# Chunked attention and a squared-ReLU feed-forward on one core: another order of the transfers in the SP queue, and of the attention steps between matmuls

## The chip, the core and the metric

The kernel runs on one core of a Trainium2 chip. The metric is the time of one execution on the device, in microseconds (us); the runs of the kernel before are 8, with a median of 291.59 us (286.88 to 293.01).

## The reference, cut to what matters

Attention is computed in chunks of 64 positions, each chunk for itself; its output, read as 4608 tokens of 512 values, goes through a feed-forward layer with a squared ReLU.

```python
# q, k, v: (8, 8, 576, 64) = batch, heads, positions, head_dim; chunk = 64
scores = matmul(q_c, k_c.T) / 8
attn = exp(scores - max(scores)); attn = attn / (sum(attn) + 1e-9)
x = matmul(attn, v_c)            # per chunk; then as (B*S, H*D) = (4608, 512)
h = maximum(x @ w_in, 0.0)       # w_in: (512, 2048)
out = (h * h) @ w_out            # w_out: (2048, 512)
```

## The kernel before

**Groups and blocks.** A group is four chunks (256 tokens), a block two groups (512 tokens): 18 groups, 9 blocks; block j holds groups 2j and 2j+1. Sixteen groups are "whole": their four chunks come from one batch row. Each batch row has nine chunks, so the ninth ones are left over, and they make groups 14 and 15 (block 7, the "rests").

**Loads** (`pieces`, L522, with `qk_pieces`, L99, and `v_pieces`, L139). A whole group's q and k come in four pieces of 256 KB (q and k of each half); a rest group's in eight of 128 KB. Its V comes as even heads (`ve_sb`) and odd heads (`vo_sb`): for a pair of whole groups 9 pieces of 64 or 128 KB, for the pair of rests 16 of 64 KB. `pieces(far)` hands out first all q and k of both groups, then all V: 17 pieces for a whole pair, 32 for the rests. All these loads are issued by SP, one after the other, and SP also issues the two kinds of DMA transposes; it goes through its queue in order, and an instruction that waits for a semaphore holds those behind it. The stores of the output are issued by POOL (L440).

**Attention of a group**, as steps that the plan places:
- C (`cast_qk`, L232): q and k cast to bf16, for these groups on ACT (L237), when their load has landed.
- TD (`transpose_qk_dma`, L239): a DMA transpose on SP, `qkT<-qkb`, 512 KB; it waits for C.
- SC (`scores`, L247): 32 small matmuls (L257) from qkT into a PSUM tile `ps_att` (two buffers), then the exponential on ACT (L264).
- AV (`values`, L267): per half of the group 16 small matmuls with V (L281) into a `ps_att` tile, then on DVE a reciprocal (L288) and a product (L289) that makes `x`.
- XT (`transpose_x`, L295): from group 6 on a DMA transpose on SP, `xT<-x`, 256 KB (L302); it waits for `x`.

**The feed-forward of a block.** `ffn_in` (L337) makes 16 tiles of `gT`, each from four matmuls 128x512 (L344) with `xT` of the block; ACT takes the ReLU (L355), DVE the square (L359), three of the 16 squares are on ACT (L357). `ffn_out` (L377) computes the second product by seven half-sized products instead of eight, in 14 halves (L412), with differences and sums on DVE (L372) and a few copies on ACT (L456, L465, L492).

**The order.** It is written out by hand, by slots. A slot is one turn of a generator: 0 to 15 the tiles of `ffn_in`, 16 to 29 the halves of `ffn_out`. While block j is multiplied, the attention of block j+1 (`nxt`) is done from SC on, and for block j+2 (`far`) the loads, C and TD. After a slot's matmuls are issued, first one more piece is loaded if the slot is in `go_slots`, then come the steps that the plan has there (`slots`); pieces that are left over are loaded at the block's end. Slots give the order in each engine's queue, not times: SP runs as far ahead as its waits allow.

Blocks 0 and 1 have plans of their own (L572 to L594). For j from 2 on (L595 to L610): one piece after each slot from 0 on; SC of both groups after slot 5, AV after 8 and 11, XT after 11 and 14, C after 18 and 22, TD after 20 and 24. Block 3 has SC after 6, AV after 9 and 12, XT after 12 and 15. Block 2 also loads the V of block 3 first (26 pieces in all), and has SC after 8 and 10, AV after 12 and 15, XT after 15 and 18, C after 20 and 23, TD after 22 and 25.

Of the kernel before, what the change touches and what calls it, by code (L numbers as in the profile page):

```python
# [17 lines left out]
def kernel(  # L18
# [80 lines left out]
    def qk_pieces(g):  # L99
        q_sb = in_pool.tile([128, 2, H, D], FP32, name="q_sb")  # L100
        k_sb = in_pool.tile([128, 2, H, D], FP32, name="k_sb")
        qk[g] = (q_sb, k_sb)
        if g < FIRST_DMA_T:
            b, s = chunks[g][0]
            for dst, src in ((q_sb, q), (k_sb, k)):
                yield lambda dst=dst, src=src, b=b, s=s: nc.sync.dma_start(
                    out=dst.rearrange("p t h d -> p (t h d)").rearrange(
                        "p (h e) -> p h e", h=H),
                    in_=src[b, :, s:s + GT, :].rearrange("h (s i) d -> s h (i d)", i=2))
            return  # L110
        for t, p, m, b, s in runs(g):
            for dst, src in ((q_sb, q), (k_sb, k)):
                yield lambda dst=dst, src=src, b=b, s=s, t=t, p=p, m=m: nc.sync.dma_start(
                    out=dst[p:p + m, t, :, :],
                    in_=src[b, :, s:s + m, :].rearrange("h s d -> s h d"))
# [23 lines left out]
    def v_pieces(g):  # L139
        for t, p, m, b, s in runs(g):  # L140
            yield lambda t=t, p=p, m=m, b=b, s=s: nc.sync.dma_start(
                out=v_even[g % NV][p:p + m, t, :, 0:D],
                in_=v[b, 0::2, s:s + m, :].rearrange("h s d -> s h d"))
        for n, p, m, b, s in odd_loads[g]:
            yield lambda n=n, p=p, m=m, b=b, s=s: nc.sync.dma_start(
                out=v_odd[n % NO][p:p + m, :, 0:D],
                in_=v[b, 1::2, s:s + m, :].rearrange("h s d -> s h d"))

    def go(pieces):
        for f in pieces:  # L150
            f()
# [163 lines left out]
    C, TD = cast_qk, transpose_qk_dma  # L315
    SC, AV, XT = scores, values, transpose_x
# [20 lines left out]
    def ffn_in(j, parts):  # L337
        if j not in gTs:
            gTs[j] = ffn_pool.tile([128, n_ft, BT], BF16, name="gT")
        gT, xT = gTs[j], xTs[j]  # L340
        for u, (c, n, ft) in enumerate((c, n, ft) for c, n, fts in parts for ft in fts):
            h = ps_ffn.tile([128, 512], FP32, name="ps_ffn")
            for dt in range(n_dt):
                nc.tensor.matmul(  # L344
                    out=h[:, 0:n],
                    lhsT=w_in_bf[:, dt, ft * 128:(ft + 1) * 128],
                    rhs=xT[:, c // 128:(c + n) // 128, dt, :],
                    start=(dt == 0), stop=(dt == n_dt - 1))
            if j < 3:
                if n == 512 or u % 2 == 0:  # L350
                    rl_tile = ffn_pool.tile([128, 512], FP32, name="rl", bufs=3).bitcast(BF16)
                rl = rl_tile[:, u % 2 * 512:] if n < 512 else rl_tile
            else:
                rl = ffn_pool.tile([128, 512], FP32, name="rl", bufs=3)
            nc.scalar.activation(out=rl[:, 0:n], in_=h[:, 0:n], func=AF.Relu)  # L355
            if (n == 512 and ft in SQUARES_ON_ACT) or (n < 512 and ft in (12, 3)):
                nc.scalar.activation(out=gT[:, ft, c:c + n], in_=rl[:, 0:n], func=AF.Square)  # L357
            else:
                nc.vector.tensor_tensor(  # L359
                    out=gT[:, ft, c:c + n], in0=rl[:, 0:n], in1=rl[:, 0:n], op=ALU.mult)  # L360
            yield
# [12 lines left out]
    def sum_quarters(out, in0, in1, op=ALU.add, half=slice(None)):  # L374
        return lambda _: add(nc.vector, out[:, half], in0[:, half], in1[:, half], op)
# [119 lines left out]
    def ffn_out_by_ft(j):  # L495

        gT = gTs.pop(j)
        n_tt = len(blocks[j]) * GT // 128
        o_ps = [ps_ffn.tile([128, d_model], FP32, name="ps_ffn") for _ in range(n_tt)]

        def mm(tt, ft):
            nc.tensor.matmul(  # L502
                out=o_ps[tt],
                lhsT=gT[:, ft, tt * 128:(tt + 1) * 128],
                rhs=w_out_bf[:, ft, :],
                start=(ft == 0), stop=(ft == n_ft - 1))

        for ft in range(n_ft - 4):
            for tt in range(n_tt):
                mm(tt, ft)  # L510
            yield
        for tt in range(n_tt):
            for ft in range(n_ft - 4, n_ft):
                mm(tt, ft)
            o_sb = ffn_pool.tile([128, d_model], FP32, name="o_sb", bufs=4)
            nc.scalar.copy(out=o_sb, in_=o_ps[tt])
            b, s0 = chunks[blocks[j][tt // 2]][0]
            t0 = b * S + s0 + tt % 2 * 128
            nc.gpsimd.dma_start(out=out[t0:t0 + 128, :], in_=o_sb)
            yield  # L520

    def pieces(grps):  # L522
        for g in grps:
            yield from qk_pieces(g)
        for g in grps:
            yield from v_pieces(g)
# [37 lines left out]
    for j, grps in enumerate(blocks):  # L564
        nxt = blocks[j + 1] if j + 1 < len(blocks) else []
        far = blocks[j + 2] if j + 2 < len(blocks) else []
        plan = {}

        def at(slot, f, g):
            plan.setdefault(slot, []).append((f, g))  # L570

        if j == 0:  # L572
            loads, go_slots = pieces(far), range(17)
            at(28, sum_quarters(b11_p_b21, b11, b21), None)
            for slot, f in ((24, TA), (27, SC), (29, AV), (31, XT)):
                at(slot, f, nxt[0])
            at(31, TQ, nxt[1])
            at(31, sum_quarters(b11_m_b22, b11, b22, ALU.subtract), None)
            phases = [ffn_in(0, [(0, 512, range(n_ft))]), ffn_out_by_ft(0)]
        elif j == 1:  # L580
            loads, go_slots = itertools.chain(*map(qk_pieces, far)), range(26, 48)
            for slot, f in ((1, TK), (4, SC), (7, AV), (12, XT)):
                at(slot, f, grps[1])
            for i, g in enumerate(nxt):
                for slot, f in ((16 + 4 * i, C), (21 + 4 * i, TD), (36 + i, SC), (38 + 2 * i, AV),
                                (41 + 2 * i, XT)):
                    at(slot, f, g)
            for i, g in enumerate(far):
                at(36 + 4 * i, C, g)
                at(42 + 3 * i, TD, g)  # L590
            at(2, sum_quarters(b11_p_b12, b11, b12), None)
            at(12, sum_quarters(b12_p_b22, b12, b22), None)
            at(20, sum_quarters(b21_p_b22, b21, b22), None)
            phases = [ffn_in(1, [(0, 256, FT_ORDER), (256, 256, FT_ORDER)]), ffn_out(1)]  # L594
        else:  # L595
            loads, go_slots = pieces(far), range(32)
            slots = {SC: (5, 5), AV: (8, 11), XT: (11, 14), C: (18, 22), TD: (20, 24)}
            if j == 3:
                slots.update({SC: (6, 6), AV: (9, 12), XT: (12, 15)})
            if j == 2:  # L600
                loads = itertools.chain(*map(v_pieces, nxt), loads)
                slots = {SC: (8, 10), AV: (12, 15), XT: (15, 18), C: (20, 23), TD: (22, 25)}
                go_slots = [*range(18), *range(26, 32)]
            for f in (SC, AV, XT):
                for i, g in enumerate(nxt):
                    at(slots[f][i], f, g)
            for f in (C, TD):
                for i, g in enumerate(far):
                    at(slots[f][i], f, g)
            phases = [ffn_in(j, [(0, BT, FT_ORDER)]), ffn_out(j)]  # L610
        slot = 0
        for phase in phases:
            for _ in phase:
                if slot in go_slots:
                    for f in loads:
                        f()
                        break
                for f, g in plan.get(slot, []):
                    f(g)
                slot += 1  # L620
        assert all(x < slot for x in plan), (j, slot, sorted(plan))
        go(loads)
# [30 lines left out]
```

## Time and profile before

| | |
|---|---|
| median of 8 runs | 291.59 us (286.88 to 293.01) |
| the profiled execution | 291.19 us, its span 289.4 us |
| PE, DVE, ACT busy in the span | 94%, 65%, 56% |
| granted TensorE clock, mean | 0.997 |
| packets on the hardware queue of SP | 47.33 MB, 76.9% of 16 engines' span |
| packets on POOL's queue (stores) | 9.18 MB, 9.7% |
| qkT by DMA: issue on SP, least / median / most | 1.4 / 2.9 / 4.4 us |
| qkT by DMA: from issue to landing | 3.9 / 5.9 / 8.7 us |
| xT by DMA: issue on SP | 1.2 / 1.3 / 3.5 us |
| xT by DMA: from issue to landing | 3.0 / 3.3 / 6.0 us |

How to read the lines of the profile. In a list of waits a line gives who waited, `<-`, for what, then the total in us, the number of times and the longest. In order of time, a line gives the start from the span's beginning, the time, the engine (SPq and ACTq are an engine's queue), the line of the kernel, the operation, output `<-` inputs, how many were merged, and in brackets the idle time before it and what ended that. A DMA's time there is that of its issue; the landing is asked for separately. The row of digits beside DMA cuts the span into 40 slices of 7.2 us, 9 being 90% busy or more.

### The profile page before, as it was taken

How to read it: one execution, taken by the hardware profiler on the slowest of the kernel's cores; microseconds unless marked ns; L12 is line 12 of the kernel's file. 1: busy time of each engine (PE TensorE's matmuls, PEld its weight loads, DVE VectorE, ACT ScalarE, POOL GpSimd, SP SyncE). 2: the span in 40 equal slices, each digit the busy share in tenths (PEclk: the TensorE clock that was granted, in tenths of full speed). 3: DMA queues.
4: the chain of work that ended last, by engine and by line, in shares of the span. 5: the costliest groups of instructions: out<-in, count | busy, mean ns of one | idle time of the engine just before them, and what ended most of it. 6: DMA issues, size and time to landing. Idle time of an engine off the chain costs nothing.

```text
span 289.4 us, 7298 instructions
## 1 busy us (share of the span) xinstructions
PE 271.0 (94%) x3011; PEld 179.8 (62%) x3014; DVE 187.8 (65%) x305; ACT 161.7 (56%) x270; POOL 54.4 (19%) x89
## 2 busy tenths in 40 slices
PE   2999999999999999799699999999999999999994
PEld 1774444788774586348544784478448844884583
DVE  1157505898943694289546974697479647965792
ACT  1527705794358654866167637763876387308710
POOL 2037733150161002000300021002000200051012
PEclk9999999999999999999999999999999999999998
DMA  7999999999999999999999999588899951132003
GB/s 204 235 332 358 321 333 251 299 217 204 215 208 268 198 191 254 194 196 206 224 247 211 200 219 269 99 154 205 235 229 192 192 164 39 39 71 75 2 18 128
DMA packets 156369, 57.10 MB, mean 197 GB/s; under 512 B 139504, under 2 KB 152048, under 8 KB 156336
## 3 DMA queue, kind: packets, MB, share of 16 engines
q1 hardware_dynamic: 153296, 47.33, 76.9%
q0 software_dynamic: 2896, 9.18, 9.7%
q8 instruction: 23, 0.38, 0.6%
q10 hardware_dynamic: 144, 0.13, 0.1%
q14 instruction: 10, 0.08, 0.1%
HBM read 36.70 MB, written 9.44 MB: 159 GB/s over the span
## 4 chain that ended last, share of the span: by engine, by line
PE 38%; DVE 5%; ACT 4%; DMA 2%; issue 2%; ACTq 0%
PE ps_ffn L412 21%; PE ps_ffn L344 16%; ACT rl L355 3%; DVE gT L359 2%; DMA xT<-x 2%; DVE x L289 2%; ACT e L264 2%; PE ps_att L281 0%; DVE rec L288 0%; DVE o_sb L492 0%; ACTq L355 0%; ACT gT L357 0%
## 5 line engine op out<-in xcount | busy, mean ns | idle before, releaser
L344 PE MATMUL ps_ffn<-xT,w_in_bf 128*128 128x512 bf16 (+1 forms) x640 | 129.8, 358 | 3.4 <-DMA xT<-x 3.2
L359 DVE TENSOR_TENSOR gT<-rl 128x512 bf16<-128x512 f32 (+2 forms) x132 | 74.4, 594 | 66.3 <-ACT rl L355 65.1
L355 ACT ACTIVATE rl<-ps_ffn 128x512 f32<-128x512 f32 (+2 forms) x160 | 85.9, 553 | 34.1 <-PE ps_ffn L344 31.2
L344 PEld LDWEIGHTS <-w_in_bf 128*128 128x128 bf16 x640 | 60.6, 98 | 60.9 <-DMA xT<-x 2.9
L412 PEld LDWEIGHTS <-w_st 128*128 128x128 bf16 x640 | 62.0, 98 | 7.6 <-DVE w_st L372 0.2
L372 DVE TENSOR_TENSOR w_st<-gT 128x2048 bf16<-128x2048 bf16 x40 | 47.3, 1218 | 0.2
L412 PE MATMUL ps_ffn<-w_out_bf,w_st 128*128 128x256 bf16 x384 | 45.1, 273 | 0.0
L440 POOL DMA_DIRECT2D out_dram<-o_sb x25 | 17.8, 714 | 132.3 <-DVE o_sb L372 127.7
L412 PE MATMUL ps_ffn<-w_sum,w_st 128*128 128x256 bf16 x256 | 29.6, 273 | 0.0
L412 PEld LDWEIGHTS <-gT 128*128 128x128 bf16 x256 | 25.0, 98 | 4.3
L289 DVE TENSOR_TENSOR x<-ps_att,rec 128x512 bf16<-128x512 f32 x36 | 24.9, 691 | 1.2
L492 ACT COPY o_sb<-ps_ffn 128x512 f32<-128x512 f32 (+1 forms) x8 | 4.5, 558 | 32.4 <-PE ps_ffn L412 32.4
L264 ACT ACTIVATE e<-ps_att 128x1024 bf16<-128x1024 f32 x18 | 17.9, 1021 | 6.6 <-PE ps_att L257 6.6
L357 ACT ACTIVATE gT<-rl 128x512 bf16<-128x512 f32 (+2 forms) x28 | 16.8, 599 | 0.9
L412 PE MATMUL ps_ffn<-w_sum,gT 128*128 128x256 bf16 x128 | 15.3, 273 | 0.0
L412 PE MATMUL ps_ffn<-w_out_bf,gT 128*128 128x256 bf16 x128 | 15.3, 273 | 0.0
L502 PE MATMUL ps_ffn<-w_out_bf,gT 128*128 128x512 bf16 x61 | 14.3, 379 | 0.6 <-ACT rl L355 0.3
L281 PEld LDWEIGHTS <-e 64*64 64x64 bf16 x576 | 6.9, 107 | 9.0 <-DVE x L289 3.5
L159 POOL CAST w_in_bf<-w_st 128x1024 bf16<-128x1024 f32 (+1 forms) x9 | 8.6, 967 | 19.6 <-DMA w_st<-in_moe_w_in_dram 19.6
L237 ACT CAST qkb<-k_sb 128x1024 bf16<-128x1024 f32 x10 | 10.5, 1046 | 1.5 <-DMA k_sb<-in_k_dram 1.5
L237 ACT CAST qkb<-q_sb 128x1024 bf16<-128x1024 f32 x10 | 10.5, 1049 | 1.4 <-DMA q_sb<-in_q_dram 1.4
L281 PE MATMUL ps_att<-ve_sb,e 64*64 64x65 bf16 x288 | 9.5, 197 | 1.9 <-DVE x L289 1.7
(52 smaller groups left out, 160.4 us busy)
## 6 DMA issues: line engine op xcount, KB each, us to landing
out_dram<-o_sb POOLq DMA_DIRECT2D x29, 256.0 KB, 4.6
q_sb<-in_q_dram SPq DMA_DIRECT2D x24, 256.0 KB, 5.1
k_sb<-in_k_dram SPq DMA_DIRECT2D x24, 256.0 KB, 4.9
ve_sb<-in_v_dram SPq DMA_DIRECT2D x32, 128.0 KB, 3.8
w_st<-in_moe_w_in_dram SPq DMA_DIRECT2D x8, 512.0 KB, 7.3
w_st<-in_moe_w_out_dram SPq DMA_DIRECT2D x8, 512.0 KB, 6.1
vo_sb<-in_v_dram SPq DMA_DIRECT2D x24, 128.0 KB, 4.0
q_sb<-in_q_dram SPq DMA_DIRECT2D x4, 512.0 KB, 6.3
```

Source lines behind the costliest of these rows:

```text
L237: copy(out=qkb[:, which], in_=qk[g][which].rearrange("p t h d -> p (t h d)"))
L264: nc.scalar.activation(out=e.rearrange("p a h t q -> p (a h t q)"), in_=ps, func=AF.Exp, scale=scale)
L281: nc.tensor.matmul(out=ps[64 * p:64 * p + 64, a, hp * (D + 1):(hp + 1) * (D + 1)], lhsT=e[64 * c:64 * c + 64, a, hp, t, :], rhs=vb[64 * c: ...
L289: nc.vector.tensor_tensor(out=x[:, t].rearrange("p h a d -> p a h d"), in0=o[:, :, :, 0:D], in1=rec.to_broadcast([128, 2, n_hp, D]), op=AL ...
L344: nc.tensor.matmul(out=h[:, 0:n], lhsT=w_in_bf[:, dt, ft * 128:(ft + 1) * 128], rhs=xT[:, c // 128:(c + n) // 128, dt, :], start=(dt == 0) ...
L355: nc.scalar.activation(out=rl[:, 0:n], in_=h[:, 0:n], func=AF.Relu)
L357: nc.scalar.activation(out=gT[:, ft, c:c + n], in_=rl[:, 0:n], func=AF.Square)
L359: nc.vector.tensor_tensor(out=gT[:, ft, c:c + n], in0=rl[:, 0:n], in1=rl[:, 0:n], op=ALU.mult)
L372: engine.tensor_tensor(out=out, in0=in0, in1=in1, op=op)
L412: nc.tensor.matmul(out=outs[t], lhsT=a[:, i, t * 128:(t + 1) * 128], rhs=b[:, i, :], start=(first and i == 0 and (last or t == 0)), stop=( ...
L440: dma.dma_start(out=out[t0:t0 + HT, col:col + HD].rearrange("(t p) d -> p t d", p=128), in_=o_sb.rearrange("p (t d) -> p t d", d=HD))
L502: nc.tensor.matmul(out=o_ps[tt], lhsT=gT[:, ft, tt * 128:(tt + 1) * 128], rhs=w_out_bf[:, ft, :], start=(ft == 0), stop=(ft == n_ft - 1))
```

## The change

The plan of blocks 2 to 8 is altered, nothing else: which slots load a piece, and after which slots SC, AV and XT stand.

```diff
         else:
-            loads, go_slots = pieces(far), range(32)
-            slots = {SC: (5, 5), AV: (8, 11), XT: (11, 14), C: (18, 22), TD: (20, 24)}
+            loads = pieces(far)
+            go_slots = [*range(8), 12, 13, 15, 16, 17, 18, 19, 21, 22, 23, 25, 26]
+            slots = {SC: (4, 4), AV: (7, 11), XT: (10, 14), C: (18, 22), TD: (20, 24)}
             if j == 3:
-                slots.update({SC: (6, 6), AV: (9, 12), XT: (12, 15)})
+                slots.update({SC: (6, 6), AV: (9, 13), XT: (12, 16)})
             if j == 2:
                 loads = itertools.chain(*map(v_pieces, nxt), loads)
                 slots = {SC: (8, 10), AV: (12, 15), XT: (15, 18), C: (20, 23), TD: (22, 25)}
-                go_slots = [*range(18), *range(26, 32)]
+                go_slots = [*range(18), 19, 20, 21, 23, 24, 26, 27, 28, 29, 30]
```

In the SP queue this gives, per block (q,k stands for pieces of q and k, V for pieces of V, XT and TD for the transposes of the two groups, with XT of the next block and TD of the one after it):

| block | before | after |
|---|---|---|
| 2, from XT(7) on | XT, TD, TD, 8 V | XT, 3 V, TD, 2 V, TD, 3 V |
| 3 | 8 q,k, 5 V, XT, 3 V, XT, 1 V, TD, TD | 8 q,k, 1 V, XT, 3 V, XT, 3 V, TD, 2 V, TD |
| 4 and 6 | 8 q,k, 4 V, XT, 3 V, XT, 2 V, TD, TD | 8 q,k, XT, 2 V, XT, 5 V, TD, 2 V, TD |
| 5 | 12 q,k, XT, 3 q,k, XT, 1 q,k, 5 V, TD, 4 V, TD, 7 V | 8 q,k, XT, 2 q,k, XT, 5 q,k, TD, 1 q,k, 2 V, TD, 14 V |

In block 7 nothing is left to load. On PE, SC of both groups moves ahead of the matmuls of one more slot in blocks 4 to 7, the first AV of those blocks too; the second AV keeps its slot there and moves one slot back in block 3.

## The prediction, made before the run

> **What bounds the kernel now.** I read the page first, then the waits of PE, then PE in order of time, and then the SP queue in order of time, because only that view says what stands ahead of what. In the page:
>
> ```profile
> PE 271.0 (94%) x3011; PEld 179.8 (62%) x3014; DVE 187.8 (65%) x305; ACT 161.7 (56%) x270; POOL 54.4 (19%) x89
> ...
> DMA  7999999999999999999999999588899951132003
> ...
> DMA packets 156369, 57.10 MB, mean 197 GB/s; under 512 B 139504, under 2 KB 152048, under 8 KB 156336
> ```
>
> PE sets the end, but the DMA engines are full until slice 25 (181 us). So until then every wait of PE for a transfer is a question of what was queued ahead of it. PE's waits after the start-up (who, us in total, times, longest):
>
> ```profile
> PE ps_ffn L344 <- DMA xT<-x: 3.2, 2, 2.7
> PE ps_att L257 <- DMA qkT<-qkb: 2.2, 2, 2.0
> PE ps_att L281 <- DVE x L289: 1.7, 4, 0.5
> ```
>
> That is 7.1 us in all, and no change of order can win more. PE in order of time places them (start, us, what, idle before):
>
> ```profile
> 112.35 6.20 PE L344 MATMUL ps_ffn<-xT,w_in_bf 128*128 128x512 bf16 x28 [0.50 <-DMA xT<-x]
> ...
> 120.89 0.45 PE L257 MATMUL ps_att<-qkT 64*64 64x64 bf16 x32 [1.96 <-DMA qkT<-qkb]
> ...
> 145.19 5.35 PE L344 MATMUL ps_ffn<-xT,w_in_bf 128*128 128x512 bf16 x24 [2.66 <-DMA xT<-x]
> ...
> 151.13 0.45 PE L257 MATMUL ps_att<-qkT 64*64 64x64 bf16 x32 [0.21 <-DMA qkT<-qkb]
> ```
>
> The L281 waits are at 157.77 (0.15) and at 186.29, 214.80 and 243.32 (0.51 each). Block 3 starts at 112.35, 4 at 145.19, 5 at 173.72, 6 at 202.24, 7 at 230.75. Last, the SP queue in blocks 5 and 6:
>
> ```profile
> 181.49 1.50 SPq L113 DMA_DIRECT2D k_sb<-in_k_dram  x1
> 186.30 1.26 SPq L302 DMA_TRANSPOSE xT<-x  x1
> 187.60 0.61 SPq L113 DMA_DIRECT2D q_sb<-in_q_dram  x1
> ...
> 199.97 1.94 SPq L243 DMA_TRANSPOSE qkT<-qkb  x1
> 201.96 2.09 SPq L141 DMA_DIRECT2D ve_sb<-in_v_dram  x3
> 204.09 2.71 SPq L145 DMA_DIRECT2D vo_sb<-in_v_dram  x4
> 206.84 1.40 SPq L113 DMA_DIRECT2D q_sb<-in_q_dram  x1
> ...
> 225.64 6.12 SPq L243 DMA_TRANSPOSE qkT<-qkb  x2
> ```
>
> SP stands still from 183.0 to 186.3, waiting for x(12); then it runs without a gap to 231.8. Asked by tile, the landing of the second transpose at 227.51 (TD(17)) comes 7.7 us later, at 235.2. SC(17) ran at about 236.3: a margin of 1.1 us.
>
> **What the Trainium skill says.** "DMA: Bandwidth & Descriptors", "Anatomy of one DMA": a semaphore wait of a DMA is served on the issuing sequencer, before dispatch; so a waiting transpose holds all that stands behind it on SP. The trace agrees (183.0 to 186.3). Same page, "Issuing engines are not separate DMA queues": transfers of SP and POOL share the 16 engines; the stores issued by POOL at 107 to 113 us stretch TD(9) to 8.7 us, where the shortest qkT landing is 3.9. Same page, "Latency and other measured facts": a DMA transpose moves 261 GB/s with a strided middle dimension; by that my estimate for 512 KB is 2.0 us, and landings of pairs here are 1.5 to 4.6 us apart, stores included. "Perfetto Trace Analysis", "DMA Instruction — HWDGE (DVE, Sync)": the shown span of a DMA is its issue, not its data movement; here a q piece issues in 0.6 to 1.2 us and lands after 5.1.
>
> **The change part by part.** (TD(g), XT(g), SC(g), AV(g): transposes of q,k and of x, scores and values of group g; block j holds groups 2j and 2j+1. Sums are made against the profiled run: span 289.4, time 291.19, so 1.8 around it; the median is 0.4 more.) No work is added or removed; all is order.
>
> Block 2. The order is the same up to XT(7) at 107.18, so the 0.50 stays. Then three V pieces go ahead of TD(8) and two more ahead of TD(9): 128+64+128+128+128 = 576 KB. Before, the eight pieces (896 KB) behind TD(9) landed from 120.9 to 126.2, or 170 KB/us: 3.4 us; at the pace of q,k (256 KB in 1.15 us) 2.6. I take 3.0. SC(9) stays at slot 6, so its wait grows from 1.96 to 5.0 and block 3 is 3.0 later: it ends at 145.5 in place of 142.5.
>
> Block 3. Each XT moves ahead of four V pieces (about 2.6 us of SP) and xT lands before 142.5. The wait of 2.66 goes; block 4 starts at 145.5, 0.3 later than now. But the same pieces (8 of q,k, 9 of V, two XT, TD(10)) stand ahead of TD(11) as now, the engines were full all along, and so it lands when it did: 145.73 + 5.4 = 151.1. SC now stands at slot 4. A slot of ffn_in costs 0.88 (5.27 / 6 in block 5). PE gets to SC(11) at 145.5 + 4.4 + 0.4 = 150.3 and waits 0.8. At 151.5 PE has done five slots, where it had done six: +0.9. The xT wait has become two qkT waits.
>
> Blocks 4 to 7. The values of the two groups stand four slots apart, not three: 0.88 more, against waits of 0.15, 0.51, 0.51, 0.51 for the PSUM buffer that DVE's x frees. They go: 1.7 us. The added square that DVE now does between the two x costs nothing, since d5 ended 0.7 before PE wanted it; with x(13) 0.5 later 0.2 is left. Block 5 then starts at 173.72 + 0.88 - 0.15 = 174.45, block 6 at 202.24 + 0.73 - 0.51 = 202.46, block 7 at 230.75 + 0.22 - 0.51 = 230.46.
>
> Block 5 loads the two groups made of rests: 16 q,k and 16 V pieces, half the size but as many issues. Now 12 q,k pieces go ahead of XT(12); after, 8. So SP runs dry at about 179 and waits for x(12) until 186.0 (AV(12) is as far behind SC as before). Four pieces (0.65 each, 2.6 us) move behind that wait. XT(13) waits for x(13) till 189.7; five pieces, then TD(14) at 194.7 to 196.1 after C(14); the last k piece goes at 196.1 and lands at about 199.1; C(15) casts it on ACT until 200.3 (ACT has nothing else due till the o_sb copy at 202.4). TD(15) waits for that: 200.3 to 201.9, landing at about 205, due at 206.8. But now 14 V pieces, not 7, stand behind it, at 0.69 (4.84 / 7): SP gets to the loads of block 6 at 201.9 + 9.6 = 211.5, not 206.84. The lag is 4.6 us.
>
> Block 6. The view by windows gives the DMA engines a share of 1.03 to 1.05 from 206.8 to 235.2: full, so a lag isn't made up, and all nine V pieces still stand ahead of TD(17). I take 4.0 of the 4.6: TD(17) lands at 239.2. The V of group 15 lands at about 214.5, AV(15) is due at 214: 0 to 0.5. SC(17), now at slot 4, is due at 230.46 + 4.4 + 0.35 = 235.2 and waits 4.0. It was at 236.3, so +2.9; one slot less done, +0.9; the last 0.5 of L281 comes off. Sum: +3.3. Span 292.7, time **294.5**.
>
> Bounds on that lag: 2.6 if only the four moved pieces count (TD(17) at 237.8, time 293.1), less by up to 1 if block 6 makes some good (292); 6.5 if TD(17) also meets more stores (241.7, time 297).
>
> **Rivals.** (a) The lag is swallowed, and TD(17) lands by 235.2. For it: TD(14) landed in 4.0 when its neighbours were V. Against: the share above 1. Then time = 291.19 + 0.22 - 0.51 - 0.51 = 290.4. (b) Faster: landings don't follow the bytes ahead, because a transpose between V pieces flows where two back to back (SP held 4.16 and 3.38 us at 141.48) block each other. Then the waits for xT at 145.19 and for qkT at 151.13 go, the one at 120.89 stays, TD(17) is in time, and all L281 waits go: 291.19 - 2.66 - 0.21 - 1.68 = 286.6. It decides where a TD with V between takes under 2 us of the engines. Against: TD(10) and TD(11) together needed only 5.1 us from 146.0 with 0.5 MB of stores among them, so there is little to win. (c) Slower still: the last k piece of group 15 lands after 201.4; C(15) then holds ACT beyond 202.4, and the o_sb copy and the first relu of block 6 wait behind it, while TD(15) and the 14 V pieces go later by the same: at 3 us more, 298. Against: 2.3 us of room.
>
> **How the numbers follow.** Wait for qkT in block 7: 0.58, 294.5, own range 292 to 297. (a) 0.20, 290.4. (b) 0.12, 286.6, give or take 1.5. (c) 0.10, 298. The range 288.5 to 297.5 leaves out most of (b) and of (c). About 2% (5.8 us) is what a measurement of this kernel can tell from no change: faster by that needs the lower third of (b), 0.04; slower is (c), 0.10; the rest, 0.86, lies within.
>
> **What would show it.** PE idle before L257 near 121 to 124 grown to about 5 us; no idle before L344 at block 4; a short L257 wait near 150; no L281 waits on DVE; SP idle for about 7 us before XT(12); the first q load of block 6 at about 211; a wait of PE of about 4 us for qkT near 235 to 239. It is wrong if the first q load of block 6 comes before 209, if that last wait is missing, or if the wait at 121 doesn't grow.

## The result, and the profile after

The changed kernel takes 302.18 us (median of 11 runs, 298.72 to 309.37); the kernel before, run beside it as well, 292.83 (32 runs). The ratio is 1.041, 95% interval 1.036 to 1.047: slower, by about three times what was forecast, and above the forecast's range of 288.5 to 297.5. Medians are over all executions, ratios leave out those that took over 1.5% longer than the fastest of the same kernel, so a ratio need not be the quotient of the medians (here 1.032). The profiled execution is one of 302.10 us with a span of 300.3, against 289.4 before: 10.9 us more.

The page of the kernel after:

```profile
PE 273.3 (91%) x3011; PEld 180.3 (60%) x3014; DVE 188.4 (63%) x305; ACT 162.5 (54%) x270; POOL 57.3 (19%) x89
...
PE   2889999999999999299999999999799939999994
...
PEclk9999999999999999689999999999999989999999
DMA  7999999999999999999999996688399970313003
```

PE has two holes, in slices 16 (120 to 128 us) and 32 (240 to 248), and the clock that PE was granted falls there, as it did in the profile of before only in the last slice. The waits of the same kernel (who, for what, us in total, times, longest):

```profile
PE ps_att L257 <- DMA qkT<-qkb: 13.3, 7, 3.7
...
PE ps_att L281 <- DMA vo_sb<-in_v_dram: 1.1, 2, 0.7
...
PE ps_ffn L344 <- DMA xT<-x: 0.6, 1, 0.6
```

Of the three waits that the change was to touch, xT fell from 3.2 to 0.6, and L281 no longer waits for DVE. The wait for qkT went from 2.2 to 13.3, of which 0.9 lie ahead of block 3. Where the rest lies, PE in order of time shows:

```profile
122.25 0.45 PE L257 MATMUL ps_att<-qkT 64*64 64x64 bf16 x32 [1.93 <-DMA qkT<-qkb]
126.43 0.64 PE L257 MATMUL ps_att<-qkT 64*64 64x64 bf16 x32 [3.73 <-DMA qkT<-qkb]
127.00 4.03 PE L344 MATMUL ps_ffn<-xT,w_in_bf 128*128 128x512 bf16 x12
...
149.30 4.48 PE L344 MATMUL ps_ffn<-xT,w_in_bf 128*128 128x512 bf16 x20
...
211.87 0.45 PE L257 MATMUL ps_att<-qkT 64*64 64x64 bf16 x32 [2.14 <-DMA qkT<-qkb]
212.24 2.76 PE L344 MATMUL ps_ffn<-xT,w_in_bf 128*128 128x512 bf16 x12
...
242.94 0.45 PE L257 MATMUL ps_att<-qkT 64*64 64x64 bf16 x32 [2.63 <-DMA qkT<-qkb]
245.41 0.51 PE L257 MATMUL ps_att<-qkT 64*64 64x64 bf16 x32 [2.03 <-DMA qkT<-qkb]
245.86 4.33 PE L344 MATMUL ps_ffn<-xT,w_in_bf 128*128 128x512 bf16 x12
```

Twelve matmuls that take 2.76 us elsewhere take 4.03 and 4.33 behind the two large waits. Block 4 starts at 149.30 with no wait. By the starts of the blocks the lengths are:

| block | before | forecast | after | after, its waits and slow matmuls |
|---|---|---|---|---|
| 3 (to the start of 4) | 32.84 | 33.15 | 35.18 | qkT 5.66, slow clock 1.3 |
| 4 | 28.53 | 28.95 | 27.78 | none |
| 5 | 28.52 | 28.01 | 27.79 | none |
| 6 | 28.51 | 28.00 | 30.96 | qkT 2.14, V 0.67 |
| 7 | 28.52 | 32.1 | 34.33 | qkT 4.66, slow clock 1.6 |
| 8 | 30.13 | 30.13 | 30.14 | none |

Block 3 starts at 114.12 after, at 112.35 before: 1.8 of the 10.9 us lie ahead of all that the change moves. The programs of the experiments below are the same up to there and start block 3 anywhere from 111.8 to 115.9, so this can't be put down to the change.

The SP queue of the kernel after, in block 5:

```profile
181.43 0.72 SPq L113 DMA_DIRECT2D k_sb<-in_k_dram  x1
188.63 1.25 SPq L302 DMA_TRANSPOSE xT<-x  x1
...
192.07 2.11 SPq L302 DMA_TRANSPOSE xT<-x  x1
...
198.17 2.55 SPq L243 DMA_TRANSPOSE qkT<-qkb  x1
200.77 0.60 SPq L113 DMA_DIRECT2D k_sb<-in_k_dram  x1
201.42 1.34 SPq L141 DMA_DIRECT2D ve_sb<-in_v_dram  x2
205.47 1.59 SPq L243 DMA_TRANSPOSE qkT<-qkb  x1
...
217.76 0.61 SPq L113 DMA_DIRECT2D q_sb<-in_q_dram  x1
```

SP stands still for 6.5 us before XT(12), again for 2.7 before TD(15), and reaches the first load of block 6 at 217.76. Block 6 starts at 204.87, so that is 12.9 us into it; before it was 206.84 against 202.24, 4.6 us into it. What SP is late by is mostly what it stood still: from the first load of block 5 to the first of block 6, its gaps of over 0.2 us come to 10.4 us here and to 3.7 before.

### The profile page after: what moved, and what is told of

The parts are those of the page before. It is cut to its first block, busy times and chain, and to the rows that moved or that the text cites. A ratio compares the mean times of both kernels' runs of the same rounds, so it can differ in the third digit from the quotient of the medians.

```text
span 300.3 us, 7292 instructions
## 1 busy us (share of the span) xinstructions
PE 273.3 (91%) x3011; PEld 180.3 (60%) x3014; DVE 188.4 (63%) x305; ACT 162.5 (54%) x270; POOL 57.3 (19%) x89
## 4 chain that ended last, share of the span: by engine, by line
PE 49%; DMA 7%; SPq 5%; DVE 1%; ACT 1%; issue 1%; ACTq 0%
PE ps_ffn L344 25%; PE ps_ffn L412 22%; DMA qkT<-qkb 4%; SPq L145 2%; DMA xT<-x 2%; SPq L141 1%; DMA k_sb<-in_k_dram 1%; PE ps_att L281 1%; SPq L243 1%; DMA vo_sb<-in_v_dram 1%; DVE w_st L372 1%; PE ps_att L257 1%; ACT rl L355 0%; DVE o_sb L372 0%; ACT n L465 0%
## 5 line engine op out<-in xcount | busy, mean ns | idle before, releaser
L344 PE MATMUL ps_ffn<-xT,w_in_bf 128*128 128x512 bf16 (+1 forms) x640 | 132.9, 363 | 1.4 <-DMA xT<-x 0.6
L359 DVE TENSOR_TENSOR gT<-rl 128x512 bf16<-128x512 f32 (+2 forms) x132 | 75.2, 599 | 76.9 <-ACT rl L355 76.0
L344 PEld LDWEIGHTS <-w_in_bf 128*128 128x128 bf16 x640 | 61.4, 99 | 61.1 <-issue 4.7
L257 PE MATMUL ps_att<-qkT 64*64 64x64 bf16 x576 | 8.5, 201 | 13.7 <-DMA qkT<-qkb 13.3
L257 PEld LDWEIGHTS <-qkT 64*64 64x64 bf16 x576 | 6.4, 113 | 19.0 <-DMA qkT<-qkb 15.2
```

The source lines that it names most:

```text
L257: nc.tensor.matmul(out=ps[64 * c:64 * c + 64, o0:o0 + 64], lhsT=qkT[64 * a:64 * a + 64, 1, t, hp, cols], rhs=qkT[64 * a:64 * a + 64, 0, t, ...
L344: nc.tensor.matmul(out=h[:, 0:n], lhsT=w_in_bf[:, dt, ft * 128:(ft + 1) * 128], rhs=xT[:, c // 128:(c + n) // 128, dt, :], start=(dt == 0) ...
L359: nc.vector.tensor_tensor(out=gT[:, ft, c:c + n], in0=rl[:, 0:n], in1=rl[:, 0:n], op=ALU.mult)
```

## The experiments

Ratios are to the kernel before, run on the same chip at the same time, with 95% intervals. "Slow stretch" means that the granted clock was at half.

**One part undone: block 5.**

```diff
             go_slots = [*range(8), 12, 13, 15, 16, 17, 18, 19, 21, 22, 23, 25, 26]
+            if j == 5:
+                go_slots = range(32)
```

> The kernel after, with the loads of block 5 (the rests) given out as before: one piece after each slot, so that 11 q,k pieces go ahead of XT(12) and half of the V ahead of TD(15). Theory (the queue order of block 5 makes SP late, and nothing later makes it good): the first q load of block 6 comes about 8 us earlier relative to the start of block 6, PE's waits for qkT in block 6 (2.1) and block 7 (4.7) and the slow matmuls after the latter (1.6) go; 302.2 - 8.4 = about 294. Rival (those waits come of SC at slot 4 and of V ahead of TD in block 6 itself): at least 4 us of them stay, 298 or more.

Measured: 295.36 us, ratio 1.003 (0.994 to 1.013). The first q load of block 6 (block 6 starts at 204.92) comes 6.1 us into it, not 12.9, and SP's gaps in the loads of block 5 come to 3.8 us, not 10.4. The first line is of SP, the others are PE's waits after block 4:

```profile
211.03 0.40 SPq L113 DMA_DIRECT2D q_sb<-in_q_dram  x1
...
211.06 0.45 PE L257 MATMUL ps_att<-qkT 64*64 64x64 bf16 x32 [1.29 <-DMA qkT<-qkb]
...
240.16 0.45 PE L257 MATMUL ps_att<-qkT 64*64 64x64 bf16 x32 [1.14 <-DMA qkT<-qkb]
```

The waits of blocks 6 and 7 fall from 7.5 us to 2.4, and no slow stretch is left there in this profile. Almost the whole loss is gone with one list of slots, though the interval still reaches to 1.013.

**One part alone: block 5 in the kernel before.**

```diff
             loads, go_slots = pieces(far), range(32)
+            if j == 5:
+                go_slots = [*range(8), 12, 13, 15, 16, 17, 18, 19, 21, 22, 23, 25, 26]
```

> The kernel before, with one thing of the change: block 5's loads in the order of the kernel after (8 q,k, XT, 2 q,k, XT, 5 q,k, TD, 1 q,k, 2 V, TD, 14 V). Theory (this order alone costs most): the first q load of block 6 comes 7 to 8 us later than now, PE waits for qkT in blocks 6 and 7 by 1 and 4 us, with 1 to 2 us of slow clock behind: before + 6.5, about 300. Rival (it is dear only together with SC at slot 4): under +3.

Measured: 301.84 us, ratio 1.038 (1.019 to 1.057), as much as the whole change. The first q load of block 6 (which starts at 204.09) comes 12.4 us into it. But the wait is another one than expected:

```profile
216.51 0.61 SPq L113 DMA_DIRECT2D q_sb<-in_q_dram  x1
...
238.61 6.96 PE L344 MATMUL ps_ffn<-xT,w_in_bf 128*128 128x512 bf16 x24 [4.12 <-DMA xT<-x]
```

Here block 6 still loads as before, with seven V pieces ahead of its second XT, so a late SP makes xT the first thing that is late. The 24 matmuls behind it take 6.96, not 5.35. By this run and the one before it, block 5's order makes SP late, and the order of block 6 chooses which transpose is late.

**Block 2 undone.**

```diff
-                go_slots = [*range(18), 19, 20, 21, 23, 24, 26, 27, 28, 29, 30]
+                go_slots = [*range(18), *range(26, 32)]
```

> The kernel after, with the loads of block 2 as before: TD(8) and TD(9) straight behind XT(7), all eight V pieces behind them. Theory: the waits for qkT in block 3 fall from 5.7 to about 2 and its matmuls keep the full clock, block 3 is 5 us shorter; SC(11) in block 4 then waits about 1 us; block 5's lag is as in the kernel after, so 302.2 - 4 = about 298. Rival (SP is the bound, so that a wait taken away in block 3 comes back in block 4): the wait for qkT(11) in block 4 is 3 us or more, 301 or more.

Measured: 301.78 us, ratio 1.027 (1.019 to 1.035). The waits for qkT in block 3 are gone altogether, and the wait in block 4, for which theory had 1 us, is 0.55 and 2.69, with a slow stretch behind it:

```profile
148.58 0.45 PE L257 MATMUL ps_att<-qkT 64*64 64x64 bf16 x32 [0.55 <-DMA qkT<-qkb]
151.71 0.64 PE L257 MATMUL ps_att<-qkT 64*64 64x64 bf16 x32 [2.69 <-DMA qkT<-qkb]
```

So in the profile the rival was right: most of the wait came back, and blocks 3 and 4 together take 61.0 us from the start of block 3 (after: 63.0; before: 61.4). In time it is open: the median is that of the kernel after, the ratio is lower (1.027, there 1.041). That the transfers bound PE up to block 4, so that their order chooses only where it waits, fits this and the profiles of all other runs: none ends block 4 before 173.2 us (before: 173.7). No run tests it by itself.

**Block 2 alone, in the kernel before**, the same two lines the other way round.

> The kernel before with one thing of the change: block 2's loads in the order of the kernel after (three V pieces ahead of TD(8), two more ahead of TD(9)). Theory (SP is the bound up to block 4, so that V ahead of TD only moves the wait): PE waits 4 to 6 us for qkT in block 3, with some slow clock behind it, but block 4's wait for xT (2.7) goes, since XT(9) lands when it did: before + 1 to 3, about 294.5. Rival (each us of V ahead of TD is lost for good): the wait for xT at block 4 stays, before + 5, 298.

Measured: 295.78 us beside 294.41 for the kernel before; there was no interval to be had for the ratio. The profile has 1.26 us for qkT in block 3, none for xT at block 4, and 0.91 and 1.08 for qkT in block 4. The wait has moved, as theory had it, but it is shorter than expected in block 3. This profile is of an execution with slow stretches in blocks 4 and 7 (mean clock 0.985), the second behind a wait of 1.74 for qkT in block 7, whose order is that of before. The other executions go from 289.16 to 297.58, so the size of this part is not settled.

**Blocks 2 and 5 undone**, both edits above.

> The kernel after with the loads of both block 2 and block 5 as before. What is left of the change: SC one slot earlier, values four slots apart, XT ahead of V in blocks 3, 4 and 6, V around TD there. Theory: these are worth the wait for xT at block 4 (2.7) and the L281 waits on DVE (1.7), less about 1 us at SC(11): 292.8 - 3.4 = about 289.5. Rival (SC at slot 4 also meets late qkT in blocks 4 and 7): 292 to 294, no better than before.

Measured: 296.47 us, ratio 1.013 (1.005 to 1.020). It came out as the rival had it, or worse: with SC at slot 4, block 4 waits 2.04 and 2.05 us for qkT and runs slow for 6.8 us behind that, and block 7 waits 2.4. What is left of the change is no gain.

**The chain through the last k piece.**

```diff
+            if j == 5:
+                go_slots = [*range(8), *range(12, 20), 21, 22, 23, 25, 26]
```

> The kernel after, with a ninth q,k slot in block 5 (a load after slot 14 too), so that all sixteen q,k pieces of the rests stand ahead of TD(14), and no piece stands between TD(14) and the cast of group 15. Theory (the last k piece, cast and TD(15) form a chain through SP that cost 2.6 us beyond the forecast): TD(15) issues about 3 us earlier, the waits of block 6 (2.1 for qkT, 0.7 for V) go, those of block 7 fall by about 2: 302.2 - 4.5 = about 297.7. Rival (SP is late by the four q,k pieces behind XT(12) and the V pieces behind TD(15), whatever stands ahead of TD(14)): no more than 1 us better, 301 or more.

Measured: 300.28 us, ratio 1.025 (0.988 to 1.061), too wide to tell from either. The profile, of the fastest of its four executions (296.58), tells more. Block 5 starts at 173.16 and TD(15) issues at 198.68, 25.5 us into it; in the kernel after it was 28.4 us. Block 6 then has no wait at all, and its first q load comes 9.4 us into it. The first line is TD(15); PE keeps the other two waits, in block 7:

```profile
198.68 1.91 SPq L243 DMA_TRANSPOSE qkT<-qkb  x1
...
235.74 0.44 PE L257 MATMUL ps_att<-qkT 64*64 64x64 bf16 x32 [2.52 <-DMA qkT<-qkb]
238.18 0.65 PE L257 MATMUL ps_att<-qkT 64*64 64x64 bf16 x32 [2.00 <-DMA qkT<-qkb]
```

So the chain made the waits of block 6, 2.8 us. They had given SP as much time: counted from the start of block 6 less these waits, SP was 10.1 us late in the kernel after and is 9.4 late here, and block 7 waits about as long (4.66 and 4.52). What is left is the wait before XT(12), where SP stands still for 5.9 us (2.7 with block 5 undone).

**The slow clock.**

```diff
                 for f, g in plan.get(slot, []):
+                    if f is SC and j in (3, 7):
+                        keep_busy(32)
                     f(g)
```

`keep_busy(n)` is the kernel's own helper: n matmuls of the identity, 128 columns each, into a PSUM tile that nobody reads; before and after use it only in their first stage.

> The kernel after, with 32 matmuls of 128x128 on the identity put ahead of each SC in blocks 3 and 7 (1.8 us each at full clock; the results go to a bank that nobody reads): PE is busy for part of the time that it waits for qkT there. Theory (the granted clock fell because PE stood idle for about 6 us, and the slow matmuls behind the wait cost 1.3 and 1.6 us beyond the wait): the clock stays at 1.00 in blocks 3 and 7, and the time falls by 2 to 3 us, to about 299.7. Rival (the clock falls for another reason, or the wait alone counts): the clock falls as before, and the time is the same or, where the extra matmuls end behind the landing, up to 2 us longer.

Measured: 299.24 us, ratio 1.017 (1.009 to 1.026), 2.9 us under the kernel after by the medians. The windows of this kernel behind the two waits (us, PE, PEld, DVE, ACT, POOL busy, granted clock, DMA share, GB/s):

```profile
127.00:131.00 4.00, 4.00 (x50) 1.83 (x48) 3.53 (x8) 2.59 (x5) 0.00 (x0) 1.00 1.01 196
...
246.00:250.00 4.00, 4.00 (x50) 1.84 (x48) 1.76 (x4) 3.23 (x6) 0.00 (x0) 1.00 0.02 4
```

and those of the kernel after:

```profile
122.80:129.60 6.80, 3.17 (x39) 1.46 (x40) 0.04 (x1) 2.60 (x3) 0.00 (x0) 0.50 1.05 219
...
245.60:249.10 3.50, 3.50 (x40) 1.39 (x29) 0.62 (x1) 1.62 (x2) 0.00 (x0) 0.51 0.02 5
```

More work on PE gave less time: the clock fell because PE stood idle. The four executions have mean clocks of 0.992 to 1.00, those of the kernel after 0.972 to 0.988. That the median fell by 2.9 agrees with the 1.3 and 1.6 us of slow matmuls, though the two were not run side by side; in the one profile part of it is given back, since block 4 waits 1.61 us for qkT.

**SC later.** The kernel with block 5 undone, and:

```diff
-            slots = {SC: (4, 4), AV: (7, 11), XT: (10, 14), C: (18, 22), TD: (20, 24)}
+            slots = {SC: (6, 6), AV: (9, 13), XT: (12, 16), C: (18, 22), TD: (20, 24)}
```

> The kernel after with the loads of block 5 as before, and SC after slot 6 (not 4), AV after 9 and 13, XT after 12 and 16 in blocks 4 to 7, as block 3 has them. Against the same kernel with SC at slot 4 (295.4, ratio to before 1.003) it asks what SC at slot 4 costs. Theory: its waits for qkT in blocks 4, 6 and 7 (1.3, 1.3, 1.1) go, each SC being due 1.8 us later: 291.5. Rival (DMA is full, each slot gained is lost at the next transpose): 294 or more.

Measured: 296.61 us, ratio 1.021 (0.999 to 1.043). In the profile blocks 4 to 7 have no wait for a transfer, as theory had it, and take 28.38 each, together 1.9 us less than in the kernel of the first experiment (113.5 and 115.4). But that is still 0.6 more a block than the 27.8 that a block without waits takes in the kernel after, and block 3, where nothing differs from the kernel of the first experiment, waited 6.4 us instead of 3.5. As a time this is inconclusive: one and the same part of the program differs by 3 us from one profile to the other.

**The values alone.**

```diff
-            slots = {SC: (5, 5), AV: (8, 11), XT: (11, 14), C: (18, 22), TD: (20, 24)}
+            slots = {SC: (5, 5), AV: (8, 12), XT: (11, 15), C: (18, 22), TD: (20, 24)}
...
-                slots.update({SC: (6, 6), AV: (9, 12), XT: (12, 15)})
+                slots.update({SC: (6, 6), AV: (9, 13), XT: (12, 16)})
```

> The kernel before with one thing of the change: the values of a block's two groups four slots apart (second AV after slot 12, in block 3 after 13) and the second XT one slot later; the loads and SC as before. Theory: the L281 waits on DVE (0.15 + 3 times 0.51) go and nothing comes in their place: 1.5 us below before, ratio about 0.995. Rival (DVE, which then has one more square between the two x, is late with d5 for the seven products): the same or slower.

Measured: 294.35 us, ratio 1.008 (1.004 to 1.012): slower. The L281 waits on DVE are gone, yet blocks 5, 6 and 7 take 28.07, 28.39 and 28.46 where they took 28.52, 28.51 and 28.52. The waits in the second half of block 6 name what came in their place:

```profile
PEld L412 <- DVE w_st L372: 0.4, 1, 0.4
```

DVE makes `x` one slot later, then the squares, then d5 (the difference that the third product multiplies), and the third product waits for it: 0.51 less, 0.4 more. (In the kernel after, with AV at 7 and 11, this doesn't show, and the gain of 0.7 a block stands.) At block 4 PE waits 4.10 us for xT, not 2.66, with a slow stretch behind it. The later slot of that XT is not the reason: it issued at 138.84 and landed at 145.3, before it was 139.16 and 145.2. PE was there earlier, because it had waited 0.56 us and not 1.96 for qkT in block 3. What that costs is the slow stretch: 24 matmuls take 6.67 us, not 5.35.

**Towards a better version.** From the kernel before:

```diff
+            if j in (3, 4, 6):
+                go_slots = [*range(8), *((14, 15) if j == 3 else (11, 12)), 17, 18, 19, 21, 22, 25, 26]
-            slots = {SC: (5, 5), AV: (8, 11), XT: (11, 14), C: (18, 22), TD: (20, 24)}
+            slots = {SC: (5, 6), AV: (7, 11), XT: (10, 14), C: (18, 22), TD: (20, 24)}
...
-                slots.update({SC: (6, 6), AV: (9, 12), XT: (12, 15)})
+                slots.update({SC: (6, 7), AV: (9, 12), XT: (12, 16)})
```

> A version that the runs so far point to, from the kernel before: blocks 2 and 5 load as before; in blocks 3, 4 and 6 the two XT go ahead of most V, and two of the nine V pieces go behind the second TD; SC after slots 5 and 6 (one group each), AV after 7 and 11, XT after 10 and 14; in block 3 SC after 6 and 7, AV after 9 and 12, XT after 12 and 16. Theory (a transpose is wanted first, V last, and no transpose may stand in SP before its input is near): the wait for xT at block 4 (2.7) shrinks to about 1 us for qkT, the L281 waits on DVE go, nothing waits in blocks 5 to 7: ratio to before 0.986, about 289. Rival (DMA is full up to block 4, so no order helps there, and the rest is under 2 us): 0.993 to 1.0.

Measured: 293.32 us, ratio 0.999 (0.994 to 1.005), as the rival had it. In its profile (mean clock 0.988) block 4 waits 1.95 and 0.99 us for qkT, followed by a slow stretch of 6.8, and blocks 5 to 7 wait 0.78 each for the exponential that AV at slot 7 needs. So the next one:

```diff
-            slots = {SC: (5, 6), AV: (7, 11), XT: (10, 14), C: (18, 22), TD: (20, 24)}
+            slots = {SC: (4, 5), AV: (7, 11), XT: (10, 14), C: (18, 22), TD: (20, 24)}
+            if j == 4:
+                slots.update({SC: (5, 6), AV: (8, 12), XT: (11, 15)})
```

> The version of the last batch, with the scores of the two groups one slot earlier in blocks 5 to 7 (after slots 4 and 5), and in block 4 the values after 8 and 12, XT after 11 and 15. Theory (its values at slot 7 stood too close behind the second scores, and PE waited 0.78 us three times for the exponential on ACT): these waits go, 2.3 us less, ratio to before 0.991. Rival (what is taken away there comes back as a wait for qkT in blocks 6 and 7): as before, 0.997 or more.

Measured: 294.73 us (288.47 to 300.53 in 6 runs) beside 292.92, with no interval to be had. The three waits of 0.78 are gone in the profile, and one of 2.52 for qkT has come in block 6. In time this is inconclusive. Last, the same with PE kept busy in block 4:

```diff
                 for f, g in plan.get(slot, []):
+                    if f is SC and j == 4:
+                        keep_busy(24)
                     f(g)
```

> The same, with 24 matmuls of 128x128 on the identity ahead of each SC in block 4 (1.35 us each at full clock; nobody reads their result), where PE waits 2 and 1 us for qkT and then runs at half clock for 6.8 us. Theory (the idle time costs more in clock than in waiting): the clock stays at 1.00 there, 1 to 2 us less than without, ratio about 0.986. Rival (the matmuls run longer than the wait, or the clock loss is small): the same or 1 us longer.

Measured: 289.20 us, ratio 0.987 (0.982 to 0.992): the one version that is faster than both kernels, by a little over 1%. Its profile has the clock at 1.00 through block 4 and no wait of PE behind 126 us; blocks 5 to 7 take 28.00 each. Block 4 takes 30.7, with 2.7 us of empty matmuls in it. How much of the gain is the clock is open, since the run without them has no interval. The single executions suggest two parts. Without the empty matmuls the one of six with a mean clock of 0.997 took 288.47, and the three of the kernel before at 1.00, run beside it, took 291.15 to 292.71: at full clock the order itself is ahead. With them all six are at 0.998 or more; five took 288.20 to 290.82, the sixth 295.94.

## Why the prediction was wrong

The sign, the place and the mechanism of the main case held: block 5's order makes SP late, block 6 doesn't make it good, and PE pays in block 7 for qkT. Its size did not: 3.3 us more were forecast, 10.9 came, of which 1.8 lie ahead of the change. Two terms failed: the chain to TD(15) in block 5, whose wait in block 6 was put at 0 to 0.5 us and measured 2.8, and the slow matmuls behind the waits, which were not in the sum and took 1.3 and 1.6. By its steps:

- **Block 2: right in the wait, blind to what follows.** 5.0 us were forecast for qkT in block 3, 5.7 came. The slow clock behind it, 1.3 us, wasn't in the sum: the profile of before has no wait over 2.7 us behind the start-up, and shows the slow clock only at its end. Other executions of that kernel do show it: the 27 beside the run with block 2 alone have mean clocks from 0.985 to 1.00.
- **Block 3 to 4: the xT wait went, as forecast; the 0.8 for qkT(11) didn't come.** TD(11) landed at 152.4 (145.36 + 7.0), but PE was so late by then that SC(11) was due only behind 153.7. Block 3 ended 2.0 us later than the step said, and block 4 gave 1.2 of it back. This fits transfers that bound PE up to block 4, as do the runs with block 2 undone and alone.
- **Blocks 4 to 7, values: right.** 27.8 a block (28.0 were forecast), without waits on DVE. It doesn't carry over to other slots: with AV at 8 and 12 or 9 and 13 a block took 28.1 to 28.5.
- **Block 5: the failed term.** XT(12) waited as forecast (6.5 us against about 7). But the last k piece was to land 24.65 us into block 5 and landed 27.3 into it (200.77 + 3.6 = 204.4), because XT(13) held SP 2.1 and not 1.3, TD(14) 2.55 and not 1.4, and the landing took 3.6 and not 3.0. TD(15) issued 28.4 us into the block, not 25.9, and landed after 6.3, not 5. The forecast's "205, due at 206.8" became 211.8, due at 209.7. Block 6 was to wait 0 to 0.5 and waited 2.8. I took the shortest issues and a quiet landing. What stretched them isn't shown; in the run with all k ahead of TD(14) the two issues took 2.08 and 2.62 all the same, and block 6 had no wait, with no k piece of group 15 behind TD(14).
- **Block 7: right in the wait, blind again to the clock.** 4.0 forecast, 4.66 came, in two parts, and 1.6 us of slow matmuls. In the runs with SC at slot 4 and no added matmuls this wait grows with how late SP is, though not one for one. Counted from the start of block 6, less what PE itself waited in block 6: 4.8 us late gives 1.1 of wait (block 5 undone), 6.7 gives 2.6 (blocks 2 and 5 undone), 9.4 gives 4.5, and 10.1 gives 4.3 (block 2 undone) and 4.7 (the kernel after).

Sum from the start of block 3, measured less forecast: +2.0, -1.2, -0.2, +3.0, +2.2, or 5.8; with the 1.8 ahead of it that is the 7.6 between 294.5 and 302.1. Rival (c) had the chain, "the last k piece lands after 201.4", one microsecond before the end of the block, and it did so (204.4, with the end at 204.87). Of the two losses that it named, TD(15) was late; PE shows no wait for ACT there. (a) is refuted: nothing was swallowed. (b) is refuted by its outcome: the waits for qkT grew. Its mechanism is not so clear: in block 3 the two TD with V between held SP for 2.05 and 2.56 us, against 4.16 and 3.38 back to back before, but in block 2 for 4.15 and 3.43, and in block 3 the second still took 7.0 to land, where it had taken 5.4.

## What to carry to other kernels

A queue that is served in order is planned by when each entry can go, not only by when it is wanted: a transpose put early in it, before its input can be there, stops every load behind, and the loads that were to fill that time have to stand ahead of it. Where transfers bound the time, another order may only move a wait, as between blocks 3 and 4 here. A wait of the matmul engine can have a second price, the slow matmuls behind it, here 1.3 and 1.6 us; don't take it as zero because one profile doesn't show it.

## What the runs showed of the hardware

The profiles show PE at half its clock behind waits for transfers, for about 3.4 or 6.8 us at a time. One wait of 4.1 us is followed by such a stretch in two runs (block 5 alone, the values alone). A single wait of 2.66 (before), of 2.68 (block 5 alone) or of 2.14 (after) isn't; one of 2.52 (the better version with SC at 4 and 5) and one of 1.74 (block 2 alone) are. Two waits close together do it as well: 2.04 and 2.05 us with a group of scores between them, 1.95 and 0.99 with scores and one slot's matmuls between, even 0.91 and 1.08. So the length of a wait alone doesn't tell. The Trainium skill, "TensorE: Matmul & The Clock Gate", "Part 1: The HAM clock gate", says that PE drops to half its clock after an idle window of about 3.4 us and needs as much activity to come back, by a window that runs freely. The lengths of the slow stretches agree with that; the waits that were enough here are shorter. The cost is the matmuls in the stretch: 12 took 4.03 us instead of 2.76.
